# Scanning every second token: decay moved into the rotation tables, and complex products summed on VectorE

## The chip, the cores and the metric

The kernel runs on one core of a Trainium2 chip. The metric is the device time of one execution in microseconds (us). The core's engines work side by side, each through its own list of instructions in order: TensorE (PE in the profile, with its weight loads as PEld), VectorE (DVE), ScalarE (ACT), GpSimd (POOL) and SyncE (SP, which here only issues transfers). Matrix products land in PSUM, and ACT or DVE copies them out into SBUF before the bank can be used again.

## The reference

The input `x` has 2048 tokens of 1024 channels. Two branches read it and a gate mixes them:

```python
g = sigmoid((x * gate_w).sum(-1, keepdims=True))          # one gate per token
# branch a: a spectral filter
a = irfft2(rfft2(x) * (w_r + 1j * w_i))                   # over tokens and channels
# branch b: a diagonal state space model with 1024 complex states
Lam_bar = exp(dt * Lam)                                   # dt = exp(log_dt), one per state
Bu = x @ B_bar.T                                          # B_bar = ((Lam_bar - 1) / Lam) * B
h[t] = Lam_bar * h[t - 1] + Bu[t]                         # 2048 steps, complex
b = 2 * real(h @ C.T) + x * Dskip
out = g * a + (1 - g) * b
```

## The kernel before

**Order of work.** Nothing is scheduled by the compiler. Every stage is a generator that issues a few instructions and yields, and the string `ORDER` (L57) names by one letter each which generator goes on next. The recurrence is cut into closures collected in `work`; the letter `v` takes the next of them, by the list `PIECES` (L44). `SLOTS` (L52) says which of four PSUM slots each product takes. So each engine's list is written out by hand, and an instruction that waits holds all that stands behind it on its engine.

**Branch b.** The 2048 tokens are eight chunks c0 to c7 of 256. For each chunk `unit_mm` (L391) makes B times x on PE, four groups per chunk, and `unit_out` (L402) copies each group on ACT into the tile `h`, which holds real and imaginary part, 8 blocks of 128 states and 256 tokens. `recur` (L334) then solves the recurrence in place on DVE. A complex decay is a rotation times a real radius: the kernel turns Bu back by the angle of each token (`cross(1)`, `along(0)`, `join_re`, `join_im`: two products with tables of sines and cosines and two sums), so that only the real radius is left, runs a first-order scan over the tokens with it (`scan`, L361, once for the real and once for the imaginary part, 8 blocks of 256 tokens in a row, with a zero radius in front of each block), and turns the result forward again with tables that also hold the factor of B_bar (`cross(3)`, `along(2)`, `out_re`, `out_im`). Between chunks three small operations carry the last state over (`carry_part`, `carry_sum`, `carry_in`). c0 and c1 are worked in two halves of four blocks each (their scans are over 1024 elements), c2 to c7 whole (2048 elements).

The tables come from `make_tab` (L272) in four steps of two blocks each: angles and their reduction on DVE or ACT, sine and cosine on ACT, casts of these into `tab` 1 and 0 on POOL or ACT, scaled copies `t1` and `t2` on ACT, and four operations on DVE that write `tab` 2 and 3. `radii` (L266) fills the scan's radii `rz` on POOL.

A finished chunk feeds `early_mm` (L732, letter n) or `own_mm` (L866, letter o): PE multiplies it with C, 128 tokens at a time, and ACT scales the result by 1 - g. The first ten token tiles go to memory and are added to the other branch there; the last ones are finished in SBUF.

**Branch a.** The transform over channels is `fold`, `fd`; over tokens it is made in two factors with a turn through memory (`s1`, `s1_store`, then `load_mid`, `s2`). `s2_out` (L599) copies the spectrum into `X2`. `times_w` (L612) multiplies it with W on DVE: for each of 8 groups and 2 halves one operation makes all four real products (W's real and imaginary part times the spectrum's). They are not summed there: `is1` (L621), the first factor of the inverse transform, sums them on PE by taking all four as inputs, with four versions of its cosines and sines in `MT`: 32 matmuls for each group, eight running at once in parts of the array. `is1_out`, `is1_store`, `load_last`, `is2` and `is2_out` (L665, into `ZT`) finish the tokens' inverse transform, and `spectral_mm` to `spectral` (L800 to L847) that over channels.

## Time and profile before

| | |
|---|---|
| median of 3 runs | 305.39 us (304.64 to 305.44) |
| span of the profiled execution | 303.6 us |
| PE busy | 296.4 us, 98% |
| DVE busy | 289.3 us, 95% |
| ACT busy | 188.5 us, 62% |
| POOL busy | 73.3 us, 24% |
| granted PE clock | 0.999 |

The profiled execution's own time is its span from the first to the last instruction; the runs are timed from outside and hold what lies around it too, 1.8 us between the two figures. A row of the profile that groups instructions reads: line, engine, operation, output <- inputs, shapes (partitions x elements, type), count | busy us, mean ns of one | idle us of the engine in front of them, and what ended it. A row of the time line reads: start, duration, engine, line, operation, and in brackets the idle time before it. Several equal instructions in a row are merged, with their count.

### The profile page before, as it was taken

What the parts mean: (1) busy time and instruction counts of PE and PEld (TensorE: products, weight loads), DVE (VectorE), ACT (ScalarE), POOL (GpSimd) and SP (SyncE); (2) the same over time, 40 slices, a digit from 0 to 9 for tenths busy, and PEclk for the clock granted to TensorE, in tenths of its full rate; (3) what the DMA queues carried; (4) which work ended last, traced back from release to release, by engine and by line L of the source; (5) the groups of instructions that cost most, each with busy time, mean ns of one, the idle gap of its engine ahead of it and who ended that gap; (6) DMA issues with size and microseconds to landing.
All of it is one profiled execution on the core that took longest, in us unless ns stands there. A gap on an engine that the chain in (4) does not pass through costs nothing. (4 is left out here: it accounts for less than half of the span.)

```text
span 303.6 us, 6402 instructions
## 1 busy us (share of the span) xinstructions
PE 296.4 (98%) x2568; PEld 197.4 (65%) x2592; DVE 289.3 (95%) x340; ACT 188.5 (62%) x255; POOL 73.3 (24%) x99
## 2 busy tenths in 40 slices
PE   8999999999999999999999999999999999999995
PEld 5664677878864685458553866669657986645543
DVE  2999999999999999999999999999899999999995
ACT  4999999896532383667665865529668774343400
POOL 2100420745893001110210220202011253252330
PEclk9999999999999999999999999999999999999999
DMA  6999999989999599895948798687758876978976
GB/s 208 341 201 194 253 193 310 162 142 154 268 214 241 160 259 219 181 250 189 212 96 258 163 223 225 139 294 147 242 174 185 165 88 135 160 132 143 165 153 181
DMA packets 74157, 59.35 MB, mean 196 GB/s; under 512 B 44904, under 2 KB 61680, under 8 KB 74128
## 3 DMA queue, kind: packets, MB, share of 16 engines
q1 hardware_dynamic: 66560, 49.82, 65.8%
q0 software_dynamic: 6912, 8.69, 23.0%
q10 hardware_dynamic: 656, 0.44, 0.5%
q8 instruction: 20, 0.33, 0.4%
q14 instruction: 9, 0.07, 0.1%
HBM read 27.46 MB, written 23.08 MB: 166 GB/s over the span
## 5 line engine op out<-in xcount | busy, mean ns | idle before, releaser
L398 PE MATMUL psu<-xQ,BT 128*128 128x256 bf16 x1024 | 116.5, 273 | 0.2 <-DVE X L449 0.2
L398 PEld LDWEIGHTS <-BT 128*128 128x128 bf16 x1024 | 99.0, 98 | 17.3 <-issue 4.6
L713 PE MATMUL ps_y<-CT,h 128*128 128x512 bf16 x397 | 92.5, 379 | 0.9
L363 DVE TENSOR_TENSOR_SCAN h<-rz,h 128x2048 bf16<-128x2048 f32 (+1 forms) x20 | 70.8, 3561 | 0.0
L713 PEld LDWEIGHTS <-h 128*128 128x128 bf16 x416 | 39.6, 98 | 46.3 <-issue 2.9
L785 POOL DMA_DIRECT2D y_scratch<-su x20 | 17.3, 902 | 135.7 <-ACT su L779 105.4
L408 ACT CAST h<-psu 128x1024 bf16<-128x1024 f32 x32 | 32.3, 1011 | 18.7 <-PE psu L398 13.1
L350 DVE TENSOR_TENSOR h<-h,tab 128x4096 bf16<-128x4096 bf16 (+1 forms) x20 | 37.1, 1859 | 0.1
L744 ACT ACTIVATE ye<-ps_y,omg 128x512 f32<-128x512 f32 x26 | 17.9, 689 | 26.3 <-PE ps_y L713 11.8
L347 DVE TENSOR_TENSOR xQ<-h,tab 128x4096 bf16<-128x4096 bf16 x12 | 27.4, 2284 | 1.0 <-ACT h L408 1.0
L603 ACT CAST X<-ps_s 128x1024 bf16<-128x1024 f32 x16 | 16.2, 1010 | 14.6 <-PE ps_s L594 11.2
L727 PE MATMUL ps_q<-CT,h 128*128 128x512 bf16 (+2 forms) x110 | 21.3, 348 | 0.2
L817 ACT ACTIVATE BT<-ps_id,gB 128x1024 bf16<-128x1024 f32 x14 | 15.3, 1114 | 9.9 <-PE ps_id L810 5.7
L671 ACT CAST ZT<-ps_is 128x1024 bf16<-128x1024 f32 x16 | 15.8, 1017 | 6.2 <-PE ps_is L661 6.2
L637 ACT CAST C<-ps_is 128x1024 bf16<-128x1024 f32 x16 | 15.7, 1011 | 5.1 <-DMA xQ<-in_A_x_dram 3.4
L851 POOL DMA_DIRECT2D BT<-y_scratch x10 | 13.1, 1452 | 19.7 <-DVE BT L846 13.3
L727 PEld LDWEIGHTS <-h 128*128 128x128 bf16 x112 | 10.3, 98 | 10.4 <-DVE h L378 0.5
L779 ACT ACTIVATE su<-xs,omg 128x512 f32<-128x512 bf16 x20 | 14.2, 723 | 4.1 <-DMA y_scratch<-su 2.2
L929 ACT COPY xQ<-pt 128x1024 bf16<-128x1024 bf16 x12 | 12.2, 1082 | 1.3 <-PE pt L919 1.3
L449 ACT CAST X<-ps_fd 128x1024 bf16<-128x1024 f32 x12 | 12.3, 1062 | 1.0 <-PE ps_fd L439 0.9
L617 DVE TENSOR_TENSOR UV<-X,Wb 128x2048 bf16<-128x2048 bf16 x8 | 9.6, 1220 | 0.6 <-ACT ye L744 0.6
L617 DVE TENSOR_TENSOR UV<-X,raw 128x2048 bf16<-128x2048 bf16 x8 | 9.8, 1223 | 0.2 <-ACT X L604 0.2
(200 smaller groups left out, 397.3 us busy)
## 6 DMA issues: line engine op xcount, KB each, us to landing
y_scratch<-ye SPq DMA_DIRECT2D x20, 256.0 KB, 4.6
y_scratch<-su POOLq DMA_DIRECT2D x20, 256.0 KB, 4.7
Bb<-turn_scratch SPq DMA_DIRECT2D x16, 256.0 KB, 5.2
turn_scratch<-C SPq DMA_DIRECT2D x16, 256.0 KB, 4.1
raw<-turn_scratch SPq DMA_DIRECT2D x8, 512.0 KB, 4.3
xs<-in_A_x_dram SPq DMA_DIRECT2D x13, 256.0 KB, 3.9
out_dram<-BT SPq DMA_DIRECT2D x11, 256.0 KB, 4.3
CT<-in_A_x_dram SPq DMA_DIRECT2D x5, 512.0 KB, 6.1
```

What stands on the lines that cost most here:

```text
L347: nc.vector.tensor_mul(out=tmps["s"], in0=u[:, ::-1], in1=bc(i))
L350: nc.vector.tensor_mul(out=u, in0=u, in1=bc(i))
L363: nc.vector.tensor_tensor_scan(out=seg, data0=rz[:, js.start + j:js.start + j + m].rearrange("p j t -> p (j t)"), data1=seg, initial=0.0, ...
L398: nc.tensor.matmul(psu[:, j, :], lhsT=BT[4 * q + j][:, ri, d8, :], rhs=xQ[:, c, d8, :], start=(d8 == 0), stop=(d8 == 7))
L408: nc.scalar.copy(out=hs[c][:, ri, 4 * q:4 * q + 4].rearrange("p b (q j) -> p b q j", j=32), in_=psus.pop((c, q, ri)).rearrange("p b (j q) ...
L603: nc.scalar.copy(out=X2, in_=ps2s[g][b])
L617: nc.vector.tensor_mul(out=UV, in0=X2s.pop((g, b)).unsqueeze(1).to_broadcast([P, 2, 2, K]), in1=fft["Wb"][g // 2 % 2][:, :, at:at + 1, :]. ...
L671: nc.scalar.copy(out=ZT[:, 4 * kp:4 * kp + 4, :, 4 * G:4 * G + 4].rearrange("p (c r) n g -> p c r n g", c=2), in_=pszs.pop((G, kp)).rearra ...
L713: nc.tensor.matmul(psy, lhsT=hs[c][:, ri, jb, P * tq:P * (tq + 1)], rhs=CT[ri][:, jb, 512 * dh:512 * (dh + 1)], start=(i == 0), stop=(i == ...
L727: nc.tensor.matmul(psq, lhsT=hs[c][:, ri, jb, P * tq:P * (tq + 1)], rhs=CT[ri][:, jb, at:at + n], start=(i == 0), stop=(i == 15))
L744: nc.scalar.activation(out=ye, in_=psys[tb][:, K * hf:K * (hf + 1)], func=ACT.Copy, scale=omg[:, tb:tb + 1])
L785: nc.gpsimd.dma_start(out=y_dram[tb, hf], in_=xgs[tb, hf], accum_op=ALU.add)
```

## The change

**Recurrence.** The tokens of a chunk are kept as 128 even ones and 128 odd ones (first index of the new `h`). The rotation tables for odd tokens are multiplied by the inverse radius on the way in and by the radius on the way out, so that a pair's two tokens need no decay between them. `fold_in` adds the even tokens to the odd ones, `scan` runs over the 128 odd tokens only, with the squared radius, and `next_` (on ACT, eight scaled copies per chunk, two to a piece) multiplies each odd result by the squared radius and writes it one place on, from where `fill_in` adds it to the next even token. The carry is put into the first place of the same buffer (`carry_in`) and added to the odd token (`carry_add`). For whole chunks real and imaginary part are now one scan of 2048 elements; for halves there are two of 512.

**Tables.** `make_tab` lets POOL cast sine and cosine of the even tokens together and multiply those of the odd ones by the inverse radius for `tab` 0 and 1, and by the radius in place for the tables 2 and 3.

**Products with W.** One operation per group makes the four products for both halves (4096 elements); a subtraction and an addition on DVE sum them, and `is1` takes the two sums: 16 matmuls a group, and `MT` keeps three versions. `X2` and `UV` are one buffer of double size instead of two.

**Layout.** Token tiles hold the even or the odd tokens of a chunk, so rows of `x` and `out`, the gate and `ZT` are laid out by that. `PIECES`, `SLOTS` and `ORDER` are written anew.

```diff
-        MT=b16(np.concatenate([-np.cos(angM), -np.sin(angM), np.cos(angM), np.sin(angM)], axis=2)),
+        MT=b16(np.concatenate([-np.sin(angM), np.cos(angM), np.sin(angM)], axis=2)),
...
     def radii():
         for jb in range(8):
-            nc.gpsimd.tensor_copy(out=rz[:, jb, :], in_=r_sb[:, jb:jb + 1].to_broadcast([P, TC]))
-            nc.gpsimd.memset(rz[:, jb, 0:1], 0.0)
+            nc.gpsimd.tensor_copy(out=rz[:, :, jb, :], in_=r2_sb[:, jb:jb + 1].unsqueeze(1).to_broadcast([P, 2, TS]))
+            nc.gpsimd.memset(rz[:, :, jb, 0:1], 0.0)
...
         yield from sincos(tmp, ang, sh, sn_f, cs_f, "rot")
         yield
-        cast(2 * jp)(out=tab[:, 1, js, :], in_=sn_f)
-        yield
+        nc.gpsimd.tensor_copy(out=tab[:, 0:2, 0, js, :], in_=sc[:, :, :, 0:TS])
+        yield
+        for j in range(2):
+            jb = 2 * jp + j
+            odd = sc[:, :, j, TS:TC]
+            nc.gpsimd.tensor_scalar_mul(out=tab[:, 0:2, 1, jb, :], in0=odd, scalar1=rinv[:, jb:jb + 1])
+            nc.gpsimd.tensor_scalar_mul(out=odd, in0=odd, scalar1=r_sb[:, jb:jb + 1])
+            yield
...
-        cast(2 * jp + 1)(out=tab[:, 0, js, :], in_=cs_f)
...
-        sh = [P, 2, n, TC]
-        u = hs[c][:, :, js, :]
+        sh = [P, 2, 2, n, TS]
+        u = hs[c][:, :, :, js, :]
...
-        def carry_in():
-            on_in.tensor_add(out=u[:, :, :, 0], in0=u[:, :, :, 0], in1=carry[:, :, js])
+        def carry_in():
+            first = tmps["s"][:, 0, :, :, 0]
+            if c:
+                nc.vector.tensor_add(out=first, in0=ck[:, :, 0, js], in1=ck[:, :, 1, js])
+            else:
+                nc.vector.memset(first, 0.0)
+
+        def carry_add():
+            nc.vector.tensor_add(out=u[:, 1, :, :, 0], in0=u[:, 1, :, :, 0], in1=tmps["s"][:, 0, :, :, 0])
+
+        def fold_in():
+            nc.vector.tensor_add(out=u[:, 1], in0=u[:, 1], in1=u[:, 0])
...
-        def scan(ri, j, m):
-            seg = u[:, ri, j:j + m].rearrange("p j t -> p (j t)")
-            nc.vector.tensor_tensor_scan(out=seg, data0=rz[:, js.start + j:js.start + j + m].rearrange("p j t -> p (j t)"),
-                                         data1=seg, initial=0.0, op0=ALU.mult, op1=ALU.add)
+        def scan():
+            flat = lambda t, i: t[:, i, js].rearrange("p j t -> p (j t)") if n < 8 else t.rearrange("p r j t -> p (r j t)")
+            for i in range(2 if n < 8 else 1):
+                seg = flat(hs[c][:, 1], i)
+                nc.vector.tensor_tensor_scan(out=seg, data0=flat(rz, i), data1=seg, initial=0.0, op0=ALU.mult, op1=ALU.add)
+
+        def next_(j):
+            for i in range(j, j + 2):
+                nc.scalar.activation(out=tmps["s"][:, 0, :, i, 1:TS], in_=u[:, 1, :, i, 0:TS - 1], func=ACT.Copy,
+                                     scale=r2_sb[:, js.start + i:js.start + i + 1])
+
+        def fill_in():
+            nc.vector.tensor_add(out=u[:, 0], in0=u[:, 0], in1=tmps["s"][:, 0])
...
         work.extend((lambda: cross(1), lambda: along(0), join_re, join_im))
+        work.append(carry_in)
         if c:
-            work.append(carry_in)
-        work.extend((lambda: scan(0, 0, n), lambda: scan(1, 0, n)))
+            work.append(carry_add)
+        work.extend((fold_in, scan))
         if c + 1 < NCH:
-            work.extend((carry_part, carry_sum))
+            work.append(carry_part)
+        work.extend(partial(next_, j) for j in range(0, n, 2))
+        work.append(fill_in)
         work.extend((lambda: cross(3), lambda: along(2), out_re, out_im))
...
     def times_w():
         for g in range(8):
-            for b in range(2):
-                UV = UVs[g, b] = fft["gt"].tile([P, 2, 2, K], BF16, name="UV", tag="guv", bufs=2)
-                at = 2 * (g % 2) + b
-                nc.vector.tensor_mul(out=UV, in0=X2s.pop((g, b)).unsqueeze(1).to_broadcast([P, 2, 2, K]),
-                                     in1=fft["Wb"][g // 2 % 2][:, :, at:at + 1, :].to_broadcast([P, 2, 2, K]))
-                yield
+            UV = UVs[g] = fft["gt"].tile([P, 2, 2, 2, K], BF16, name="UV", tag="guv", bufs=1)
+            W = fft["Wb"][g // 2 % 2][:, :, 2 * (g % 2):2 * (g % 2) + 2]
+            nc.vector.tensor_mul(out=UV, in0=X2s.pop(g).unsqueeze(1).to_broadcast([P, 2, 2, 2, K]),
+                                 in1=W.unsqueeze(2).to_broadcast([P, 2, 2, 2, K]))
+            yield
+            nc.vector.tensor_sub(out=UV[:, 0, 0], in0=UV[:, 0, 0], in1=UV[:, 1, 1])
+            yield
+            nc.vector.tensor_add(out=UV[:, 0, 1], in0=UV[:, 0, 1], in1=UV[:, 1, 0])
+            yield
...
     def is1():
         for g in range(8):
             psc = pscs[g] = [psum([P, 2, K], "ps_is1") for _ in range(2)]
-            UV = [UVs.pop((g, b)) for b in range(2)]
-            for i, (u, r, n) in enumerate(((0, 0, 64), (0, 1, 32), (1, 0, 32), (1, 1, 0))):
+            UV = UVs.pop(g)
+            for r in range(2):
                 for c in range(4):
                     rows = slice(32 * c, 32 * (c + 1))
                     for b in range(2):
-                        nc.tensor.matmul(psc[c // 2][64 * b:64 * (b + 1), c % 2, :], lhsT=fft["MT"][rows, 2 * g + b, n:n + 64],
-                                         rhs=UV[b][rows, u, r, :], start=(i == 0), stop=(i == 3), tile_position=(32 * c, 64 * b))
+                        nc.tensor.matmul(psc[c // 2][64 * b:64 * (b + 1), c % 2, :], lhsT=fft["MT"][rows, 2 * g + b, 32 - 32 * r:96 - 32 * r],
+                                         rhs=UV[rows, 0, r, b, :], start=(r == 0), stop=(r == 1), tile_position=(32 * c, 64 * b))
             yield
...
+        nc.scalar.activation(out=r2_sb, in_=are, func=ACT.Exp, scale=2.0)
+        nc.scalar.activation(out=rinv, in_=are, func=ACT.Exp, scale=-1.0)
```

The cosines' factor in `rot` (the carry) takes the squared radius too, and the exponent of the radius is kept from below -60 ln 2 so that its inverse stays finite.

The new order between a scan and its `fill_in`, on DVE: in c2 the product with W of group 3 and `along(0)` of c3, with small sums; in c3 `cross(1)` and `along(0)` of c4 and the product of group 5; in c4 the same of c5 and the product of group 7; in c5 `cross(1)`, `along(0)` and both joins of c6; in c6 `cross(3)` and `along(2)` of c5; in c7 eight operations of the spectral sums. On ACT the `next_` pieces of c6 stand behind four copies of `is2`.

151 lines of the change are left out of this document (75 added, 76 removed), and 13 rows, old and new, of the table PIECES.

## The prediction

> **What bounds the kernel now.** I read the totals of the page first, then the busy time in five stretches whose bounds are events of the kernel: the tables finish at about 80 us, the products with W run from 104.7 to 188.8, the row-wise inverse transform from 188.8, the spectral sums from 241. The columns are PE, PEld, DVE, ACT, POOL, then granted clock, DMA share, GB/s.
>
> ```profile
> PE 296.4 (98%) x2568; PEld 197.4 (65%) x2592; DVE 289.3 (95%) x340; ACT 188.5 (62%) x255; POOL 73.3 (24%) x99
> ...
> 0.00:80.00 80.00, 77.20 (x691) 56.85 (x695) 72.27 (x136) 69.92 (x98) 26.14 (x56) 1.00 1.10 218
> 80.00:104.70 24.70, 24.54 (x193) 15.10 (x193) 24.04 (x33) 7.15 (x12) 12.29 (x8) 1.00 0.93 213
> 104.70:188.80 84.10, 83.73 (x837) 52.34 (x829) 83.30 (x66) 54.79 (x79) 8.69 (x10) 1.00 0.85 208
> 188.80:241.00 52.20, 51.94 (x466) 37.34 (x470) 51.15 (x33) 33.44 (x42) 6.86 (x8) 1.00 0.75 191
> 241.00:303.60 62.60, 58.98 (x403) 35.73 (x407) 58.58 (x77) 23.19 (x26) 19.28 (x18) 1.00 0.82 146
> ```
>
> Two engines are full at once. PE is idle for 303.6 - 296.4 = 7.2 us, 2.8 of it in the first stretch and 3.6 in the last; DVE for 14.3 us. The clock is 1.00 throughout, so PE's time is work. ACT has 115 us free, but only 10 of the first 80. The chain of waits shows the same balance: it runs through DVE's last chunk of the recurrence, then through PE to the end.
>
> ```profile
> 285.42 1.15 DVE h L378
> ...
> 286.61 5.79 PE ps_q L727 x26
> ...
> 292.44 7.99 PE ps_q L727 x52
> ...
> 300.46 0.35 DVE raw L899
> ```
>
> So a microsecond taken from PE alone, or from DVE alone, is not necessarily a microsecond off the end. What both lose counts.
>
> **The price list for DVE.** Rows of single instructions include about 0.09 us in which the next one already runs. The true step is the second instruction of a pair: the merged pair less the single.
>
> ```profile
> L363 DVE TENSOR_TENSOR_SCAN h<-rz,h 128x2048 bf16<-128x2048 f32 x12 | 52.7, 4416 | 0.0
> L363 DVE TENSOR_TENSOR_SCAN h<-rz,h 128x1024 bf16<-128x1024 f32 x8 | 18.1, 2278 | 0.0
> L350 DVE TENSOR_TENSOR h<-h,tab 128x4096 bf16<-128x4096 bf16 x12 | 27.4, 2287 | 0.0
> L617 DVE TENSOR_TENSOR UV<-X,raw 128x2048 bf16<-128x2048 bf16 x8 | 9.8, 1223 | 0.2 <-ACT X L604 0.2
> L617 DVE TENSOR_TENSOR UV<-X,Wb 128x2048 bf16<-128x2048 bf16 x8 | 9.6, 1220 | 0.6 <-ACT ye L744 0.6
> L846 DVE TENSOR_TENSOR BT<-BT 128x1024 bf16<-128x1024 bf16 x7 | 4.7, 684 | 0.0
> ```
>
> ```profile
> 73.61 4.46 DVE L363 TENSOR_TENSOR_SCAN h<-rz,h 128x1024 bf16<-128x1024 f32 x2
> ...
> 148.37 2.34 DVE L617 TENSOR_TENSOR UV<-X,Wb 128x2048 bf16<-128x2048 bf16 x2
> ...
> 175.20 8.74 DVE L363 TENSOR_TENSOR_SCAN h<-rz,h 128x2048 bf16<-128x2048 f32 x2
> ...
> 191.51 4.49 DVE L350 TENSOR_TENSOR h<-h,tab 128x4096 bf16<-128x4096 bf16 x2
> ...
> 278.92 1.29 DVE L846 TENSOR_TENSOR BT<-BT 128x1024 bf16<-128x1024 bf16 x2
> ```
>
> Scan of 2048: 8.74 - 4.42 = 4.32. Scan of 1024: 4.46 - 2.28 = 2.18; by the line through both, a scan of 512 is 1.11. Two-tensor bf16 operation: 4096 elements 4.49 - 2.29 = 2.20; 2048 1.12; 1024 1.29 - 0.69 = 0.60. An element of a scan costs four times one of a sum, which is what the change trades on.
>
> **Recurrence, DVE.** Six chunks (c2 to c7) run whole. Each loses two scans of 2048 and gets one, and adds fold_in and fill_in over 2048 elements: -4.32 + 2 x 1.12 = -2.08, six times -12.5. The first two run in halves, four in all: two scans of 1024 become two of 512 and two sums of 1024 are added: -2 x 2.18 + 2 x 1.11 + 2 x 0.60 = -0.94, four times -3.8. The four table products and four joins keep their element counts; their innermost runs stay contiguous, so I keep their price. The carry keeps three small operations (new: into the first column, add, part). Recurrence: -16.3 us.
>
> **Products with W, DVE.** Sixteen products of 2048 go, 16 x 1.12 = 17.9. Eight products of 4096 with a subtraction and an addition of 1024 each come, 8 x (2.20 + 2 x 0.60) = 27.2. That is +9.3 us, all in the stretch 104.7 to 188.8, where only about three chunks (-2 each) repay it. DVE over the whole kernel: -16.3 + 9.3 = -7.0 us, but in that stretch it is about +3.
>
> **PE.** is1 issues half its matmuls, since the complex sum is already made.
>
> ```profile
> L629 PE MATMUL ps_is<-UV,raw 32*64 32x512 bf16 x256 | 8.6, 380 | 0.0
> ...
> 132.92 1.07 PE L629 MATMUL ps_is<-UV,raw 32*64 32x512 bf16 x32
> ```
>
> Eight tiles run side by side, so 32 matmuls take 1.07 us; half are 0.5, and eight groups save 8.6 / 2 = 4.3. Halved groups may keep a fixed edge (1.07 contains one matmul's 0.38 of latency): 8 x 0.5 = 4.0 is the other bound. I take -4.2. No other matmul changes in count or size.
>
> **ACT.** The 64 instructions of next_ scale 254 elements each; nearest row: a scaled copy of 256. Its pair gives 0.94 - 0.54 = 0.40, single 0.54. Three casts go to POOL.
>
> ```profile
> L292 ACT ACTIVATE t<-sn_f,ci 128x256 f32<-128x256 f32 x8 | 3.8, 543 | 0.0
> ...
> L294 ACT CAST tab<-cs_f 128x512 bf16<-128x512 f32 x2 | 1.2, 610 | 0.0
> ...
> L287 ACT CAST tab<-sn_f 128x512 bf16<-128x512 f32 x1 | 0.6, 617 | 0.0
> ```
>
> ```profile
> 45.36 0.94 ACT L292 ACTIVATE t<-sn_f,ci 128x256 f32<-128x256 f32 x2
> ```
>
> 64 x 0.40 = 25.6, less 1.8: +24 us (+33 by the single). ACT goes to about 212 us, 70%; in the stretch of the W products from 54.8 to about 66 of 84. It fits; the cost is not its sum but the new hand-off: scan (DVE), next_ (ACT), fill_in (DVE). One chunk's eight take 3.3 us. In the written order DVE has work between scan and fill_in: in c2 to c5 at least two products of 4096 (4.4 us) and sums besides; in c7 four of the spectral sums and some more, about 4 us. Cover is thus 1 us or more in most chunks, nearly nothing in c6 and c7, where next_ stands behind copies of PSUM. If those two slip by 0.4 us each, that is 0.8. If the cover were gone everywhere, 8 x 3.3 = 26 us. What waits behind a next_ that itself waits for the scan is the copying of h, X, C and ZT out of PSUM, and so PE's next free bank.
>
> **POOL and the tables.** Each of the four table steps gets one cast of 1024 elements and four products of 256; five casts of 512 go.
>
> ```profile
> L268 POOL COPY rz<-r_sb 128x256 f32<-128x256 f32 x8 | 4.5, 559 | 0.3 <-ACT r_sb L1091 0.3
> ...
> L287 POOL CAST tab<-sn_f 128x512 bf16<-128x512 f32 x3 | 2.4, 805 | 24.0 <-ACT sn_f L1111 24.0
> ...
> L294 POOL CAST tab<-cs_f 128x512 bf16<-128x512 f32 x2 | 1.2, 614 | 0.9 <-ACT cs_f L1113 0.9
> ```
>
> A product of 256 by the copy of 256 (scaled ones are not in the trace): 0.56, sixteen 9.0; four casts of 1024 at twice 0.6: 4.8; less 3.6: +10 us of POOL. It has the room, but the chain is longer: ACT's t1 and t2, DVE's last four table operations and cross1 now all stand behind POOL, about 3.4 us per table. And POOL does not run freely beside DVE:
>
> ```profile
> 86.38 1.21 DVE L350 TENSOR_TENSOR h<-h,tab 128x2048 bf16<-128x2048 bf16 x1
> 87.52 2.27 DVE L363 TENSOR_TENSOR_SCAN h<-rz,h 128x1024 bf16<-128x1024 f32 x1
> ...
> 90.90 2.27 DVE L347 TENSOR_TENSOR xQ<-h,tab 128x4096 bf16<-128x4096 bf16 x1
> 93.40 0.19 DVE L557 CAST Zp<-zps 128x32 bf16<-128x32 f32 x1 [0.23 <-PE zps L553]
> ```
>
> ```profile
> 86.39 6.90 POOL L540 TENSOR_TENSOR AB<-Wh 128x32 f32<-128x32 f32 x1
> ```
>
> A POOL sum of 32 elements started with DVE's L350 and ended 6.9 us later, when DVE paused at 93.2. The other way, DVE pays: its sum of 1024 beside two POOL operations took 1.11 instead of 0.68.
>
> ```profile
> 30.10 0.68 DVE L943 TENSOR_TENSOR preT<-xQ 128x1024 bf16<-128x1024 bf16 x1
> 30.70 1.11 DVE L945 TENSOR_TENSOR sums<-xQ 128x1024 bf16<-128x1024 bf16 x1
> ```
>
> ```profile
> 30.65 0.61 POOL L287 CAST tab<-sn_f 128x512 bf16<-128x512 f32 x1 [11.45 <-ACT sn_f L1111]
> ```
>
> The Trainium skill, "SBUF — State Buffer", section "Who interferes with whom", says why: a DVE instruction with two SBUF inputs and a POOL instruction that reads SBUF exclude each other for a whole instruction. These rows agree. By that rule taken in full, POOL's 10 us more would be 10 us of DVE, and the change would cost DVE 3 us instead of saving 7.
>
> From rows: for two POOL operations (0.61 + 0.86) DVE lost 0.43, a third; of 10 us that makes about 3; bounds 0 and 10. The loss falls before 80 us. There the order leaves PE cover: the first matmul of the output (n) stands behind all of c0 and also behind DVE's first six operations of c1a (two products, two joins, fold, scans: about 6.5 us). So I put no PE time on it, and DVE's balance at -7.0 + 3 = -4.0, about PE's -4.2.
>
> **Layout moves.** Splitting even and odd tokens in h, ZT and the rows of x and out changes strides, not counts: h is read by PE in runs of 128 as before, the copies keep 1024 elements, each DMA row stays 2 KB. The three transposes of x stand far ahead of their use. I price all of these at nothing, bound -0.5 to +1.5 us. X2 and UV become one buffer each instead of two halves, so the product of group g+1 waits until is1 of g is done; the order puts a scan or other DVE work between, and is1 takes 0.5 us.
>
> **The sum.** The execution profiled spans 303.6 us; the median of the runs is 305.39, 1.8 more, taken as fixed. PE -4.2, hand-offs +0.8: 303.6 - 3.4 = 300.2 span, 302.0 as a time.
>
> **Rivals.**
> (1) Both engines gain more: with DVE ahead, PE's inner idle shrinks too. DVE's last write starts at 300.46 and the span ends at 303.6, so about 3.2 of PE's 7.2 idle us are the tail; if two thirds of the other 4.0 vanish and hand-offs cost nothing, 305.4 - 4.2 - 2.6 = 298.6. For it: DVE is the last to release in the chain. Against: three new hand-offs.
> (2) DVE sets the pace in the W stretch, and POOL's claim on it is paid in full in the table stage: two thirds to all of the 10 us leave DVE with -0.3 to +3, and if PE then only follows DVE, 305.1 to 308.4; nearest the low end, 305.5, since part of the table stage's DVE work reads PSUM. For it: L540. Against: the third that the row at 30.70 gives, and the 6.5 us of PE's cover.
> (3) The other side: ACT's next_ blocks. ACT works in order; next_ cannot start before the scan ends, and copies out of PSUM stand behind it, so PE loses its banks. There are ten scan units (four halves, six chunks). From 4.2 / 10 = 0.42 us of PE lost per unit it eats the whole gain, from 0.51 it is slower. With one single next_ pair of lateness per unit, 0.94 us: 305.4 - 4.2 + 9.4 = 310.6; with 0.7, 308.2. For it: PE at 98% has no time to lose. Against: ACT has 115 us free.
> (4) The change does not do what it says: the 4096 product with W repeats each input by a broadcast and could run at half rate, 8 x 2.20 = 17.6 us more on DVE in its tightest stretch: about 315. The old product has the same kind of broadcast at 1220 ns for 2048, so hardly.
>
> **How the numbers follow.** Forecast 302.0 (with 300.5 to 304 around it): 0.56. Rival 1, 298.6: 0.12. Rival 2, 305.5: 0.16. Rival 3, 308: 0.14. Rival 4: 0.02. About 0.3% (0.9 us) is what a measurement of this kernel can tell from no change. Faster takes the forecast and rival 1 and some of rival 2: 0.71. Same: most of rival 2, 0.13. Slower: rivals 3, 4 and the upper end of 2, 0.16. The range runs from rival 1's 298.6 to 306.5, above rival 2 and short of most of rival 3.
>
> **What would show it.** PE's busy time near 292 and is1 near 4.3 us; six scans of 2048 and eight of 512 elements, together about 36 us instead of 70.8; products with W at 2.3 us each; PE idle no more than about 8 us. ACT's waits for DVE h in front of next_, and PE's waits for ACT behind them, show rival 3; long POOL products and DVE waiting for POOL before 80 us show rival 2. I am wrong if PE's idle time grows by more than 3 us.

## The result: 3.5% slower, and the profile after

| | before | after |
|---|---|---|
| median of the runs shown | 305.01 us (304.54 to 305.44) | 315.95 us (314.75 to 317.05) |
| ratio | | 1.0349, 95% interval 1.0310 to 1.0387 |
| span of the profiled execution | 303.6 us | 313.9 us |

The forecast was 302.0 us in a range of 298.6 to 306.5: wrong in sign. In e9 and e10 below one run of ten (345.77 us at a granted clock of 0.853, 306.52 us at 0.994) is left out of median and ratio. First the totals of the page after, with PE's busy tenths and granted clock in 40 slices:

```profile
span 313.9 us, 6252 instructions
...
PE 298.3 (95%) x2464; PEld 197.3 (63%) x2464; DVE 287.7 (92%) x364; ACT 212.5 (68%) x318; POOL 83.0 (26%) x114
...
PE   8999799978999999997999999999999999999994
...
PEclk9999979999999999999999999999999999999999
```

PE's idle time was 303.6 - 296.4 = 7.2 us and is now 313.9 - 298.3 = 15.6. DVE's went from 14.3 to 26.2. The work itself hardly changed: PE +1.9, DVE -1.6. Of the 10.3 us, 8.4 are waiting on PE's side. (PE's busy time did not fall by what is1 lost. Some matmuls ran at a lower clock, below, and the trace of before lacks 24 of its 2592 matmul records: e9's trace, with the same work on PE and all records, has PE busy for 298.1 us and idle for 6.0.) The same five stretches as in the prediction, of the kernel after (PE, PEld, DVE, ACT, POOL, clock, DMA share, GB/s):

```profile
0.00:80.00 80.00, 71.30 (x616) 51.23 (x616) 64.49 (x129) 63.73 (x94) 40.39 (x66) 0.98 1.02 207
80.00:104.70 24.70, 24.70 (x201) 16.80 (x200) 23.94 (x39) 13.65 (x22) 7.59 (x12) 1.00 0.84 185
104.70:188.80 84.10, 81.84 (x720) 50.87 (x719) 80.21 (x77) 58.38 (x94) 8.70 (x10) 1.00 0.87 210
188.80:241.00 52.20, 52.20 (x433) 34.44 (x431) 51.55 (x37) 41.60 (x65) 6.02 (x7) 1.00 0.74 194
241.00:313.90 72.90, 68.27 (x503) 43.98 (x500) 67.46 (x86) 35.17 (x46) 20.28 (x19) 1.00 0.79 142
```

In the first 80 us PE did 71.30 us of work instead of 77.20, and DVE 64.49 instead of 72.27. From 80 to 241 us PE is never idle but for one hole between 104.7 and 188.8: what is lost early has no room to be made up later.

The groups that the change touches:

```profile
L370 DVE TENSOR_TENSOR_SCAN h<-rz,h 128x2048 bf16<-128x2048 f32 x6 | 26.5, 4420 | 0.1
L370 DVE TENSOR_TENSOR_SCAN h<-rz,h 128x512 bf16<-128x512 f32 x8 | 9.3, 1209 | 0.1
L634 DVE TENSOR_TENSOR UV<-X,raw 128x4096 bf16<-128x4096 bf16 x4 | 9.1, 2280 | 0.2 <-PE ps_is L650 0.2
L650 PE MATMUL ps_is<-UV,raw 32*64 32x512 bf16 x128 | 5.1, 386 | 0.0
L374 ACT ACTIVATE xQ<-h,r_sb 128x254 bf16<-128x254 bf16 x48 | 20.5, 505 | 6.6 <-DVE h L370 6.6
L291 POOL TENSOR_SCALAR tab<-sc,rinv 128x256 bf16<-128x256 f32 x8 | 10.5, 1307 | 0.0
L292 POOL TENSOR_SCALAR sc<-sc,r_sb 128x256 f32<-128x256 f32 x8 | 9.6, 1197 | 0.8
L299 ACT ACTIVATE t<-sc,ci 128x256 f32<-128x256 f32 x16 | 7.3, 503 | 7.7 <-POOL sc L292 7.7
L303 DVE SCALAR_TENSOR_TENSOR tab<-sc,cr,t 128x256 bf16<-128x256 f32 x8 | 4.0, 505 | 4.0 <-ACT t L299 4.0
```

The change does what it says: the scans take 35.8 us instead of 70.8, is1 5.1 instead of 8.6. What is out of line are the products on POOL, 1.2 to 1.3 us each, and the column behind the second bar: ACT waited 7.7 us for them, and DVE 4.0 us for ACT. How that reaches PE is seen in the time line of one table step, first POOL, then ACT, then PE:

```profile
31.64 0.61 POOL L286 CAST tab<-sc 128x512 bf16<-128x512 f32 x1 [7.44 <-ACT sc L1139]
32.23 1.36 POOL L291 TENSOR_SCALAR tab<-sc,rinv 128x256 bf16<-128x256 f32 x1
33.69 0.97 POOL L292 TENSOR_SCALAR sc<-sc,r_sb 128x256 f32<-128x256 f32 x1
34.64 1.82 POOL L291 TENSOR_SCALAR tab<-sc,rinv 128x256 bf16<-128x256 f32 x1
36.56 0.92 POOL L292 TENSOR_SCALAR sc<-sc,r_sb 128x256 f32<-128x256 f32 x1
37.43 0.40 POOL L267 COPY rz<-r_sb 128x256 f32<-128x256 f32 x1
```

```profile
34.70 0.51 ACT L299 ACTIVATE t<-sc,ci 128x256 f32<-128x256 f32 x1 [0.31 <-POOL sc L292]
37.52 1.31 ACT L299 ACTIVATE t<-sc,ci 128x256 f32<-128x256 f32 x3 [2.31 <-POOL sc L292]
38.73 0.99 ACT L491 CAST CT<-ps_s 128x1024 bf16<-128x1024 f32 x1
```

```profile
33.58 3.67 PE L412 MATMUL psu<-xQ,BT 128*128 128x256 bf16 x32
37.08 0.38 PE L991 MATMUL ps_r<-preT,JP_sb 128*128 128x512 bf16 x1
39.77 5.32 PE L412 MATMUL psu<-xQ,BT 128*128 128x256 bf16 x32 [2.31 <-ACT CT L491]
```

POOL's chain of one cast and four products lasts from 31.64 to 37.48, 5.8 us. ACT's second scaled copy stands 2.31 us for its last product; behind it in ACT's list stands a copy out of PSUM (L491) that has nothing to do with tables; PE needs that bank and stands 2.31 us too. The next 32 matmuls then took 5.32 us, where the 32 before the wait took 3.67: another 1.65. Two of the other three table steps do the same to PE: at 66.42 us it has stood 1.92 us for a copy L491, and at 78.07 us 1.34 us for a copy L463, each behind scaled copies that waited for POOL (1.67 and 2.14 us).

The second hole, between 136 and 149 us, runs through a store. ACT's copy C waits for the place of an earlier store to memory, and the shifted copies of c2 stand behind it:

```profile
139.15 0.90 ACT L374 ACTIVATE xQ<-h,r_sb 128x254 bf16<-128x254 bf16 x2
143.48 1.01 ACT L658 CAST C<-ps_is 128x1024 bf16<-128x1024 f32 x1 [3.42 <-DMA turn_scratch<-C]
144.38 0.91 ACT L374 ACTIVATE xQ<-h,r_sb 128x254 bf16<-128x254 bf16 x2
```

```profile
144.54 3.65 PE L412 MATMUL psu<-xQ,BT 128*128 128x256 bf16 x32 [1.05 <-ACT C L658]
149.05 7.15 PE L412 MATMUL psu<-xQ,BT 128*128 128x256 bf16 x64 [0.85 <-ACT X L621]
```

DVE's `fill_in` of c2 starts at 148.13 after 3.06 us of idling for them. PE stands 1.05 us for the copy C and 0.85 us for the copy X that is behind the shifted ones.

### The profile page after: what moved, and what is told of

It reads as the page before. It is cut to its first block, busy times and chain, and to the rows that moved or that the text cites. A ratio compares the mean times of both kernels' runs of the same rounds, so it can differ in the third digit from the quotient of the medians.

```text
span 313.9 us, 6252 instructions
## 1 busy us (share of the span) xinstructions
PE 298.3 (95%) x2464; PEld 197.3 (63%) x2464; DVE 287.7 (92%) x364; ACT 212.5 (68%) x318; POOL 83.0 (26%) x114
## 4 chain that ended last, share of the span: by engine, by line
PE 43%; ACT 12%; issue 12%; DVE 12%; POOL 10%; DMA 8%; SPq 1%; POOLq 0%; ACTq 0%; DVEq 0%
PE psu L412 18%; PE ps_y L734 15%; PE ps_q L748 6%; POOL tab L291 3%; ACT xQ L950 3%; POOL sc L292 2%; DVE h L345 2%; DVE xQ L342 2%; DMA y_scratch<-su 2%; DMA turn_scratch<-C 2%; DMA BT<-y_scratch 2%; DMA out_dram<-BT 2%; ACT X L463 2%; DVE h L370 1%; PE ps_s L611 1%
## 5 line engine op out<-in xcount | busy, mean ns | idle before, releaser
L412 PE MATMUL psu<-xQ,BT 128*128 128x256 bf16 x1024 | 117.8, 275 | 6.5 <-ACT CT L491 2.3
L412 PEld LDWEIGHTS <-BT 128*128 128x128 bf16 x1024 | 100.2, 99 | 24.9 <-issue 11.9
L734 PE MATMUL ps_y<-CT,h 128*128 128x512 bf16 x416 | 93.6, 379 | 0.0
L806 POOL DMA_DIRECT2D y_scratch<-su x20 | 19.7, 996 | 129.2 <-ACT su L800 101.3
L370 DVE TENSOR_TENSOR_SCAN h<-rz,h 128x512 bf16<-128x512 f32 (+1 forms) x14 | 35.9, 2585 | 0.2
L374 ACT ACTIVATE xQ<-h,r_sb 128x254 bf16<-128x254 bf16 x48 | 20.5, 505 | 6.6 <-DVE h L370 6.6
L692 ACT CAST ZT<-ps_is 128x1024 bf16<-128x1024 f32 x16 | 16.7, 1127 | 3.0 <-PE ps_is L683 3.0
L838 ACT ACTIVATE BT<-ps_id,gB 128x1024 bf16<-128x1024 f32 x14 | 15.1, 1113 | 5.2 <-PE ps_id L831 3.8
L748 PEld LDWEIGHTS <-h 128*128 128x128 bf16 x112 | 10.3, 98 | 11.0 <-issue 0.7
L299 ACT ACTIVATE t<-sc,ci 128x256 f32<-128x256 f32 x16 | 7.3, 503 | 7.7 <-POOL sc L292 7.7
L342 DVE TENSOR_TENSOR su<-h,tab 128x2048 bf16<-128x2048 bf16 x8 | 9.8, 1228 | 2.9 <-POOL tab L291 2.8
```

The costliest lines, as they stand in the source:

```text
L342: nc.vector.tensor_mul(out=tmps["s"], in0=u[:, :, ::-1], in1=bc(i))
L370: nc.vector.tensor_tensor_scan(out=seg, data0=flat(rz, i), data1=seg, initial=0.0, op0=ALU.mult, op1=ALU.add)
L374: nc.scalar.activation(out=tmps["s"][:, 0, :, i, 1:TS], in_=u[:, 1, :, i, 0:TS - 1], func=ACT.Copy, scale=r2_sb[:, js.start + i:js.start + ...
L412: nc.tensor.matmul(psu[:, j, :], lhsT=BT[4 * q + j][:, ri, d8, :], rhs=xQ[:, c, d8, :], start=(d8 == 0), stop=(d8 == 7))
L692: nc.scalar.copy(out=fft["ZT"][:, kp, :, :, 2 * G:2 * G + 2], in_=pszs.pop((G, kp)).rearrange("p v (x n) -> p x n v", n=64))
L734: nc.tensor.matmul(psy, lhsT=hs[c][:, tq, ri, jb, :], rhs=CT[ri][:, jb, 512 * dh:512 * (dh + 1)], start=(i == 0), stop=(i == 15 and tb not ...
```

## The experiments

### Which engine sets the pace?

The prediction counted on both PE and DVE. So work was taken from each alone in the kernel before, then from both, and from DVE in the kernel after.

```diff
 e8 (before, is1)
-            for i, (u, r, n) in enumerate(((0, 0, 64), (0, 1, 32), (1, 0, 32), (1, 1, 0))):
+            for i, (u, r, n) in enumerate(((0, 0, 64), (0, 1, 32))):
 e9 (before) and e16 (after), mul_skip; e10 = e8 and e9 together
-                nc.vector.tensor_mul(out=xs[tb], in0=xs[tb], in1=fft["Db"])
```

> The kernel before with half of is1's matmuls left out (the products with W's imaginary part are not added), 16 instead of 32 for each group, and nothing else changed: PE's gain of the change by itself, without anything on DVE. Theory PE (PE sets the pace, the step of the prediction that counted -4.2 us): 300.5 to 301.5 us. Theory DVE (DVE sets the pace, as the kernel with only W changed says: 9.8 us more on DVE, 8.6 us more in all): 304.3 to 305.5, no change.

> The kernel before with the 13 VectorE products of x by Dskip left out (that part of the output is missing), nothing else: VectorE loses 7.8 us, spread from 160 to 230 us, TensorE loses nothing. Theory A (VectorE sets the pace of the kernel before): about 298. Theory B (TensorE sets it): 305. Theory C (both are full and each stretch is set by whichever is late there): between, about 302, since the half of is1's products left out of TensorE gave 2.7 of its 4.

> The kernel before with both cuts at once: half of is1's matrix products and all 13 products by Dskip left out. Theory C: more than the two alone together, because where one engine is freed the other one was the limit: 305 less 2.7 less what the Dskip products gave alone, less some 1 to 3 us more, about 297 to 299. Theories A and B: the sum of the two alone, no more.

> The kernel after without the 13 VectorE products by Dskip (that part of the output is missing): VectorE loses 7.8 us between 160 and 230 us. If VectorE sets the pace of the kernel after behind the tables: 308 to 311. If TensorE does, as in the kernel before: within 1.5 us of 316.

| | median | ratio to before |
|---|---|---|
| e8: PE loses half of is1 | 302.96 us | 0.9909 (0.9879 to 0.9940) |
| e9: DVE loses 13 products | 305.90 us | 1.0036 (1.0001 to 1.0072) |
| e10: both | 302.11 us | 0.9889 (0.9866 to 0.9912) |
| e16: after, DVE loses 13 products | 315.24 us | 1.0332 (1.0292 to 1.0371) |

The result is e9's theory B, that PE sets the pace, for both kernels; e8 alone came out between its two theories. Is1's group of matmuls went from 8.6 to 5.6 us in e8, and 0.0091 x 305.7 = 2.8 us came off the end: nearly one for one. DVE's row in e9 says 282.3 us busy instead of 289.3, and nothing came off; both cuts together gave 0.0111 x 305 = 3.4 us, no more than PE's alone within the intervals. In e16 DVE's 7.6 us less bought nothing either. These products lie between 160 and 230 us, so this shows that DVE's sum of work is not a bound there; it does not show that DVE may be late anywhere (below).

### The products on POOL

```diff
 e1 (after): the odd rows are only cast
-        for j in range(2):
-            nc.gpsimd.tensor_scalar_mul(out=tab[:, 0:2, 1, jb, :], in0=odd, scalar1=rinv[:, jb:jb + 1])
-            nc.gpsimd.tensor_scalar_mul(out=odd, in0=odd, scalar1=r_sb[:, jb:jb + 1])
+        nc.gpsimd.tensor_copy(out=tab[:, 0:2, 1, js, :], in_=sc[:, :, :, TS:TC])
 e5 (after): the products on DVE, all four of a table where POOL's last stood
-            nc.gpsimd.tensor_scalar_mul(out=tab[:, 0:2, 1, jb, :], in0=odd, scalar1=rinv[:, jb:jb + 1])
-            nc.gpsimd.tensor_scalar_mul(out=odd, in0=odd, scalar1=r_sb[:, jb:jb + 1])
+            nc.vector.tensor_scalar_mul(out=tab[:, 0:2, 1, jb, :], in0=odd, scalar1=rinv[:, jb:jb + 1])
+            nc.vector.tensor_scalar_mul(out=odd, in0=odd, scalar1=r_sb[:, jb:jb + 1])
```

> The changed kernel with its 16 scaled products on POOL left out: the odd half of the first two tables is only cast (four casts of 512 elements), so the decay inside a pair is left out of all four tables. Everything else, the order too, is that of the changed kernel (315.95 us). Theory POOL (the loss is made before 85 us, by products that take 0.92 to 1.98 us each and hold ACT's t1, the copies out of PSUM behind it, and so PE): PE's idle time between 28 and 82 us (about 8 us) and the 1.7 us of a slowed clock go, so 306 to 308 us. Theory ACT (the loss is next_ and its hand-offs): the stall before 85 us is a side show that later slack takes up, 314 to 316. Theory W (the extra sums of the products with W on DVE set the pace of the middle): same, 314 to 316.

> The changed kernel with the 16 scaled products of the tables made by DVE in place of POOL, all four of a table step at the place of the last POOL product; nothing is left out. DVE pays 16 times about 0.27 us (the spacing of its scaled copies of 256 elements), 4.3 us, before 75 us. Theory POOL: 308 to 311, since the wait goes and DVE's 4.3 us come, part of them in time that DVE stood waiting. Theories ACT and W: 315 to 319, since DVE has more to do and nothing else changes.

e1: 310.8 us, ratio 1.0154 (1.0078 to 1.0231). e5: 315.54 us, ratio 1.0312 (1.0237 to 1.0386). The stretch from 28 to 82 us in the kernels before, after, e1 and e5, one fence each:

```profile
28.00:82.00 54.00, 53.81 (x492) 42.73 (x491) 52.89 (x80) 46.52 (x68) 24.06 (x39) 1.00 1.12 211
```

```profile
28.00:82.00 54.00, 47.66 (x415) 37.03 (x413) 45.00 (x74) 42.28 (x65) 30.72 (x40) 0.97 1.01 190
```

```profile
28.00:82.00 54.00, 52.31 (x479) 41.84 (x477) 51.77 (x82) 48.33 (x73) 18.30 (x33) 1.00 1.05 213
```

```profile
28.00:82.00 54.00, 48.96 (x439) 38.24 (x438) 51.75 (x92) 45.37 (x69) 12.54 (x28) 1.00 1.05 201
```

Without the products PE works 4.65 us more in this stretch, the clock is back at 1.00, and the end comes (1.0349 - 1.0154) x 305 = 5.9 us earlier by the ratios (5.2 by the medians). That is about half of the loss (a third to four fifths within the intervals), and it is shown; the expectation of 306 to 308 us had counted on more. None of the three waits of PE behind scaled copies is left in e1's trace: from 28 to 82 us PE stands only for two loads, 1.12 us for c_T and 0.49 us for B. DVE hardly gains: with 3.6 us of casts in place of 20.1 us of products on POOL it is busy for 287.3 us instead of 287.7.

Moving the products to DVE (e5) did not give the 308 to 311 us expected of it. In its trace ACT waits for them 2.9 us instead of 7.7, and PE's waits for the copies L492 behind them are 0.63 us each, where the copies L491 of after had cost 2.31 and 1.92. But a product takes 0.45 us on DVE, not the 0.27 expected, and DVE is busy for 4.6 us more. PE does 48.96 us of work in the stretch, still 4.85 less than before, and its longest wait is now another, 1.84 us for the load of c_T. So e5 took away most of the chain's waits and paid for it elsewhere; it does not tell the chain's length from the engine that holds it.

### The shifted copies on ACT

```diff
 e2 (after), e12 (e1) and e18 (e17): the copies left out
-        work.extend(partial(next_, j) for j in range(0, n, 2))
+        work.extend((lambda: None) for j in range(0, n, 2))
 e17 (e1): the letter L, the load of K, moved in ORDER
-YccvncvLsyM
+YLccvncvsyM
```

> The changed kernel without next_: the 64 scaled copies on ACT are left out, so fill_in adds what the buffer holds and the even tokens lack their predecessor's state. Theory POOL: the 27 us of ACT time are mostly hidden; only the 3 us stall at 145 us and small change go, 312 to 316. Theory ACT: the hand-off is the loss, 304 to 307. Theory W: 314 to 316.

> The kernel after without the 16 scaled POOL products (odd rows of the tables only cast) and without ScalarE's 64 shifted copies (the even rows take in a stale buffer): both suspected hand-offs are gone, the output is not the reference's. If what was left of the loss with the products out (310.8) is the shifted copies': 305 to 307. If the engines' fullness and the order set it: within 1 us of 310.8.

> The kernel after without POOL's 16 scaled products, with the load of K issued ahead of the last three transposing transfers of C before it. If that load's place only mattered in the run without shifted copies: 310.8 as with the products out alone. If the load's place cost something there too: 308 to 310.

> The same, and without ScalarE's 64 shifted copies. If the shifted copies and their hand-offs hold the rest of the loss: 305 to 307, 3 us or more under the kernel with them. If they cost nothing, as with the products in: within 1.5 us of the kernel with them; the rest of the loss then belongs to the order of work, and is not settled further.

e2: 316.13 us, ratio 1.0352 (1.0268 to 1.0435): 64 copies, 24 us of ACT and every hand-off from the scan to ACT gone, and no time with them. PE's work from 110 to 150 us rose from 37.74 to 39.16, so the second hole closes for the most part, but the end does not move: 1.1 us of this is lost again near the end, where PE's wait for ACT's copy BT (L838) grew from 0.6 to 1.7 us.

e12, with the products gone too, took 313.22 us (ratio 1.0249, 1.0188 to 1.0310), no better than e1. The trace of its slowest run (315.1 us) shows a stall of its own: first SyncE's queue, then PE.

```profile
85.45 5.05 SPq L720 DMA_TRANSPOSE CT<-in_B_C_im_dram  x1
90.55 1.31 SPq L720 DMA_TRANSPOSE CT<-in_B_C_re_dram  x1
92.03 0.45 SPq L511 DMA_DIRECT2D K_sb<-c_K  x1
```

```profile
94.78 0.36 PE L567 MATMUL zps<-Bcol,K_sb 32*128 32x32 bf16 x8 [2.67 <-DMA K_sb<-c_K]
96.41 0.37 PE L608 MATMUL ps_s<-Bb,KRS_sb 64*32 64x512 bf16 x1 [1.27 <-DMA Bb<-turn_scratch]
97.34 1.05 PE L608 MATMUL ps_s<-Bb,KRS_sb 64*32 64x512 bf16 x15 [0.56 <-DMA Bb<-turn_scratch]
```

A transposing transfer of C took 5.05 us to issue, its neighbours 1.3; the small load of K stood behind it, and PE stood 4.5 us in all. With that load put ahead, e17 took 312.04 us (1.0209, 1.0145 to 1.0273) and e18 310.72 us (1.0189, 1.0118 to 1.0260): the same within the intervals. So no share of the rest of the loss is shown for the shifted copies, though up to about 3 us could hide in this noise.

### The products with W

```diff
 e4 (before, its own order): one pair tile of one buffer, the sums, 16 matmuls a group
+            UV = UVs[g] = fft["gt"].tile([P, 2, 2, 2, K], BF16, name="UV", tag="guv", bufs=1)
...
+                if b == 1:
+                    nc.vector.tensor_sub(out=UV[:, 0, 0], in0=UV[:, 0, 0], in1=UV[:, 1, 1])
+                    nc.vector.tensor_add(out=UV[:, 0, 1], in0=UV[:, 0, 1], in1=UV[:, 1, 0])
 e14 (before): the pair tile without the sums, 32 matmuls a group
+            UV = UVs[g] = fft["gt"].tile([P, 2, 2, 2, K], BF16, name="UV", tag="guv", bufs=1)
 e15 (before): two buffers; for each product its own two sums, 16 matmuls
+                if g >= 4:
+                    nc.vector.tensor_sub(out=UV[:, 0, 0], in0=UV[:, 0, 0], in1=UV[:, 1, 1])
+                    nc.vector.tensor_add(out=UV[:, 0, 1], in0=UV[:, 0, 1], in1=UV[:, 1, 0])
 e13: as e15 in all groups, with nc.gpsimd for nc.vector
```

> The kernel before with only the products with W changed: the four products as before in two operations of 2048 elements, behind the second of them the subtraction and the addition on DVE, and 16 matmuls instead of 32 for each group. The order is that of before. DVE gets 16 x 0.60 = 9.6 us more between 104 and 189 us, PE 3.5 to 4.2 us less. If DVE sets the pace in that stretch (theory W): 311 to 315 us. If PE sets it: 301 to 302. If both do in turn, as theory POOL needs for the middle of the changed kernel: 306 to 311.

> The kernel before with the two products of a group of W in one tile of a single buffer, as the sums would need it, but without the sums: 32 matrix products for a group as before. VectorE and TensorE work as before. If the single buffer caused the loss of 8.6 us of the products with W alone: 309 to 314. If VectorE's added work caused it: 305 to 306.

> The kernel before with VectorE's complex sums only in the last four of the eight groups, each of the two products of a group with its own buffer and its own two sums (512 elements, by my estimate from 0.69 us for 1024 about 0.37 us each, +6 us of VectorE), and 16 instead of 32 matrix products in those groups (half of the 2.7 us that the removed products gave). If VectorE has the slack that leaving out the Dskip products showed: 303.5 to 305. If VectorE's work counts in full: 308 to 311.

> The kernel before with the complex sums in all eight groups made by POOL (32 operations of 512 elements, estimated at 1 to 2 us each from its scaled products of 0.92 us for 256 and its casts of 1.04 for 1024), two buffers, 16 matrix products a group. VectorE's work is as before. If only VectorE's work mattered: 302 to 304. If the delay in the chain to the products or POOL's claim on SBUF matters: 306 to 315.

| | median | ratio to before |
|---|---|---|
| e4 | 313.65 us | 1.0250 (1.0172 to 1.0329) |
| e14 | 305.32 us | 0.9997 (0.9983 to 1.0012) |
| e15 | 310.51 us | 1.0166 (1.0122 to 1.0210) |
| e13 | 344.35 us | 1.1262 (1.1245 to 1.1280) |

The single buffer costs nothing (e14). DVE's sums cost, in the order of before: half of them add 5.9 us to DVE (289.3 to 295.2) and 0.0166 x 305.6 = 5.1 us to the end, although PE has less to do. The rows of before and of e15 for the stretch from 150 to 210 us, and PE's wait in e15:

```profile
150.00:210.00 60.00, 59.68 (x571) 39.25 (x562) 59.20 (x40) 35.80 (x53) 7.76 (x9) 1.00 0.76 196
```

```profile
150.00:210.00 60.00, 55.23 (x452) 34.41 (x442) 59.76 (x53) 31.41 (x47) 6.01 (x7) 0.97 0.76 183
```

```profile
L635 PE MATMUL ps_is<-UV,raw 32*64 32x512 bf16 x192 | 8.2, 402 | 4.4 <-DVE UV L620 4.4
```

DVE was full there before, 59.20 of 60, and is full now; what it does more, PE waits for (4.4 us in front of is1). In the same stretch and later, taking DVE work away bought nothing (e9). DVE's full stretch has slack in one direction only. The sums also stand between a product and the is1 that needs it; whether DVE's fullness or this place in the chain makes PE wait, e4 and e15 do not separate. And the wait belongs to the order of before: in after's trace PE never waits for UV, so e4's loss is no part of after's.

On POOL the sums are far worse (e13, expected at 315 us at most):

```profile
L621 POOL TENSOR_TENSOR UV<-UV 128x512 bf16<-128x512 bf16 x16 | 43.5, 2716 | 0.0
L620 POOL TENSOR_TENSOR UV<-UV 128x512 bf16<-128x512 bf16 x16 | 39.4, 2465 | 37.5 <-DVE UV L617 23.7 <-DMA raw<-c_MT 12.4 <-DVE carry L371 1.4
```

In the mean that is 2.5 and 2.7 us for 512 elements, where DVE took 0.42 in e15; single ones took 1.15 to 5.27. PE waited 25.5 us for them (18.3 and 7.2). DVE, with the same work as before, was busy for 312.8 us instead of 289.3, beside 80 us more of POOL (153.7 instead of 73.3).

### The recurrence alone

```diff
 e3 (after): the products with W and is1 undone, the order of after
-            nc.vector.tensor_mul(out=UV, in0=X2s.pop(g).unsqueeze(1).to_broadcast([P, 2, 2, 2, K]),
-                                 in1=W.unsqueeze(2).to_broadcast([P, 2, 2, 2, K]))
+            for b in range(2):
+                nc.vector.tensor_mul(out=UV[:, :, :, b], in0=X2[:, :, b].unsqueeze(1).to_broadcast([P, 2, 2, K]),
+                                     in1=W[:, :, b:b + 1].to_broadcast([P, 2, 2, K]))
...
-            for r in range(2):
+            for i, (u, r, n) in enumerate(((0, 0, 64), (0, 1, 32), (1, 0, 32), (1, 1, 0))):
 e6 (e3): POOL's products left out as in e1
 e7 (e3): complete tables; DVE scales the odd rows, POOL makes 8 products
+            nc.vector.tensor_scalar_mul(out=odd, in0=odd, scalar1=r_sb[:, jb:jb + 1])
...
-        nc.scalar.activation(out=rinv, in_=are, func=ACT.Exp, scale=-1.0)
+        nc.scalar.activation(out=rinv, in_=are, func=ACT.Exp, scale=-2.0)
 e11 (e7): ORDER, PIECES and SLOTS of before; all shifted copies of a chunk in
 one piece; in half chunks DVE operations in their place
+                for i in range(n):
+                    nc.vector.scalar_tensor_tensor(out=u[:, 0, :, i, 1:TS], in0=u[:, 1, :, i, 0:TS - 1],
+                                                   scalar=r2_sb[:, js.start + i:js.start + i + 1], in1=u[:, 0, :, i, 1:TS],
+                                                   op0=ALU.mult, op1=ALU.add)
```

> The changed kernel with the products with W undone: two products of 2048 elements for each group, no subtraction or addition, 32 matmuls of is1 and four versions of its table; recurrence, tables, layout and order are those of the changed kernel (315.95 us). DVE gets about 10 us less, PE 3.5 to 4.2 more. Theory DVE: 306 to 308 us. Theory PE: 318 to 320. If the order's other hand-offs set the pace: 313 to 316.

> As the kernel with only the recurrence changed, and the 16 scaled products of the tables on POOL left out too (the odd half is only cast, so the decay inside a pair is missing from the tables): the recurrence's worth without its tables' price. Theory DVE: 10 us below the changed kernel without these products (310.8), 300 to 303, and below before. Theory PE: 313 to 315.

> As the kernel with only the recurrence changed, with the tables complete but built otherwise: DVE multiplies the odd half by the radius in place (8 products, about 0.3 us each, +2.4 us), and POOL makes the first two tables from that with the inverse radius squared (8 products instead of 16), so that ACT's t1 and t2 no longer wait for POOL. Nothing is left out. Theory DVE: between the two others, 303 to 306: POOL's share of the wait is halved and DVE pays 2.4 us. If POOL's products still hold DVE at cross1 as long as before: 306 to 309.

> The recurrence over odd tokens with complete tables (VectorE multiplies the odd half by r, POOL makes 8 scaled products), in the order of work of the kernel before: its list of issues, its list of recurrence pieces and its PSUM slots; the products with W as before. In the four half chunks the shifted addition is 16 VectorE operations with a scalar in place of ScalarE's copies, as the second buffer does not fit there. Nothing is left out. Theory order (the loss of 8.7 us seen with the same tables and the order of after comes from the order being fitted to other costs): 301 to 306. Theory operations (the work of the change itself, hand-offs and small dependent VectorE operations, costs it): 310 to 315. VectorE busy about 285 in both.

| | median | ratio to before |
|---|---|---|
| e3 | 318.60 us | 1.0423 (1.0369 to 1.0476) |
| e6 | 314.85 us | 1.0286 (1.0235 to 1.0336) |
| e7 | 314.35 us | 1.0284 (1.0230 to 1.0338) |
| e11 | 342.26 us | 1.1198 (1.1151 to 1.1246) |

With DVE at 279.5 us in e3, ten less than before, the kernel is 2.7 us slower than after by the medians, with intervals that overlap a little. That fits an order in which PE's matmuls of is1 count, as in e8, and DVE's relief does not. Splitting the table products between DVE and POOL (e7) is worth as much as leaving them out (e6). e6 came out where PE's pace had put it, e7 above both of its ranges (303 to 309 us). e11 failed as a test of a better home for the recurrence, but it shows what after's order is for. Its waits:

```profile
ACT xQ L374 <- DVE h L370: 19.4, 4, 7.3
DVE xQ L342 <- ACT h L445: 11.0, 3, 6.3
DVE h L378 <- ACT xQ L374: 9.8, 2, 7.0
```

The shifted copies put where the second scan stood make ACT wait 19.4 us in four places; copies out of PSUM stand behind them, and DVE stands 11.0 us for those. PE's idle time was 341.5 - 310.5 = 31 us. e11 also differs in the half chunks and in the tables' place in the list, so it does not price the shifted copies alone.

## Why the prediction was wrong, step by step

**"A product of 256 by the copy of 256: 0.56."** This is the step that failed first. The scaled products took 0.92 us at the least and 1.25 in the mean; their starts in the time line, 0.87 to 1.92 us apart, say the same, while the copies of 256 in the same trace took 0.39 to 0.83, 0.57 in the mean. The chain of a table, put at 3.4 us, took 5.3 to 7.0. The copy was the wrong neighbour, and no other was looked for. (The cast in this chain was counted with 1024 elements; it has 512 and took 0.78 us in the mean instead of 1.2, so the products lost more than the chain shows.) POOL's total rose by 9.7 us, as forecast, but by luck: products and casts are 19.6 us more, and the rest of POOL's work happened to take 9.9 us less, 4.5 of it in one sum of 32 elements (L557, 2.4 us where L540 had 6.9).

**"So I put no PE time on it."** This is the step that cost most. The cover that was named, the output matmuls behind DVE's first operations of c1, was the wrong place to look. The late tables reached PE by ACT's list: the scaled copies t1 and t2 wait for POOL, and unrelated copies out of PSUM stand behind them. e1 gives the price, 5 to 6 us where nothing had been put. The prediction had named just this path for the shifted copies (rival 3) and not for t1 and t2, which stand in the same list.

**"PE -4.2, hand-offs +0.8."** The products explain 5.2 us of the 14 between forecast and result; e1, without them, is still 8.8 us above the forecast. The sum had 0.8 us for all new waits of PE, and the new order of the whole had no term at all. In e1's trace PE's waits with a named cause add up to 7.8 us, in before to 2.7. New are 2.0 us in the second hole for the copies C and X, 1.6 for the loads of c_T and B, 0.5 for Bb, and 1.5 near the end for ACT's copy BT, which itself waits 1.96 us for an earlier store to out.

**"What both lose counts."** PE's part held in the main: -4.2 was forecast, is1 gave 3.5 us in after's trace, and e8 shows that such a cut comes off the end nearly one for one. DVE's part did not: 7.0 us off DVE were worth nothing by themselves (e9), so DVE's balance was no ground for a gain; and DVE's +9.3 in the W stretch was a danger that a balance over the whole kernel hid, though it came true only in the order of before (e4: +7.6 us by its ratio, e15: +5.1). In after's order the recurrence's relief does lie beside the sums: undoing them (e3) costs 2.7 us by the medians.

**DVE -7.0.** It came as -1.6. The large terms were right: scans -35.0 against -34.5, the products with W 9.1 + 9.1 + 5.5 + 5.5 = 29.2 for 19.4, +9.8 against +9.3. `fold_in` and `fill_in` came to 20.2 us by their rows, where 18.2 had been taken; the other 3.4 us were not traced to single operations. A part of both is the step that was taken from pairs that overlap. Two sums of `fold_in`, each with the operation behind it, all with POOL idle:

```profile
191.15 1.22 DVE L364 TENSOR_TENSOR h<-h 128x2048 bf16<-128x2048 bf16 x1
192.40 4.42 DVE L370 TENSOR_TENSOR_SCAN h<-rz,h 128x2048 bf16<-128x2048 f32 x1
...
216.27 1.22 DVE L364 TENSOR_TENSOR h<-h 128x2048 bf16<-128x2048 bf16 x1
217.41 0.68 DVE L790 TENSOR_TENSOR xs<-xs,Db 128x1024 bf16<-128x1024 bf16 x1
```

The scan at 192.40 reads what `fold_in` wrote and starts 1.25 us behind it; the product at 217.41 does not and starts 1.14 us behind, near the 1.12 of the price list.

**POOL beside DVE.** The third that the prediction took for DVE's loss is near what e13 shows: 23.5 us of DVE for 80 us of POOL. In the table stage, where it was put at 3 us, e1's 0.4 us shows next to nothing. The Trainium skill, "SBUF — State Buffer", section "Who interferes with whom", has the two exclude each other for whole instructions when DVE has two SBUF inputs; the direction agrees, but DVE did not pay POOL's full time here.

**Rival 1** fell with the sign: PE's idle time grew instead of shrinking. **Rival 2** (the table stage and DVE's late stretch) named the right place with the wrong mechanism, POOL's claim on DVE instead of its delay of ACT. **Rival 3** did not decide after (e2), since its order leaves room between scan and `fill_in`, as the prediction reckoned; it shows only in c2, behind a store (the second hole). e11 shows that the waits are long without that room, together with its other changes. **Rival 4** is refuted: 2.28 us for 4096 elements. **Layout**: the pair tile costs nothing (e14); the rest was not tried alone. The sign that was named for being wrong, PE's idle time growing by more than 3 us, is what the trace shows: +8.4.

**What stays open.** With the products out and the load of K in either place the kernel is still 1.5 to 2.1% slower than before, though is1's cut is in it. It is not shown to be the shifted copies (e18) and, with the products still in, not DVE's work from 160 to 230 us (e16). Where it lies is seen in e1's trace, in the waits named above. Without the shifted copies (e18) the wait for C and X falls from 2.0 to 0.5 us, and three others grow: c_T to 2.0, Bb to 1.2, BT to 2.0. Why these loads, stores and copies come late is not shown: that the new order of the whole fits less well than the old one is likely, but no run isolates it. No kernel with all of the computation in it beat the kernel before; e14 came level with it.

## What to carry to other kernels

Where two engines are both near full, find out which one's work comes off the end before trading work between them: here a microsecond off PE was worth 0.9, one off DVE nothing, and one more on DVE in its full stretch, in front of is1, 0.9. Price a step moved to another engine by its place in the lists, not by the room on that engine: what waits for it, and what unrelated work stands behind the waiter. An operation that the trace doesn't hold needs a bound from a neighbour of its own kind; here the copy bounded the scaled product only from below.

## What the runs showed of the hardware that was not expected

- POOL's product of 256 fp32 elements with one factor per partition took 0.92 to 1.98 us, a copy of the same size 0.39 to 0.83; its sum of two bf16 tiles of 512 elements, beside a DVE busy for 91% of the span, took 1.15 us at the least and 2.5 to 2.7 in the mean, DVE's 0.42.
- After a wait of 2.31 us PE ran slower for a while: 32 matmuls in 5.32 us instead of 3.67. After one of 1.92 us it did not. The length of the wait alone does not decide it: in e4, 64 matmuls took 8.83 us after a wait of 2.73 and 7.16 after one of 2.66. The two windows of after with these waits (clock third from the end), and the second wait:

```profile
40.00:50.00 10.00, 10.00 (x76) 7.55 (x74) 7.59 (x14) 7.00 (x12) 6.90 (x9) 0.83 1.09 205
60.00:70.00 10.00, 8.08 (x74) 6.55 (x71) 8.46 (x16) 7.05 (x14) 4.80 (x8) 1.00 1.06 199
```

```profile
66.42 3.65 PE L412 MATMUL psu<-xQ,BT 128*128 128x256 bf16 x32 [1.92 <-ACT A L491]
```

The Trainium skill, "TensorE: Matmul & The Clock Gate", section "Why this matters for your kernels", warns of idle gaps above about 3 us; here a lower clock followed one of 2.31 us already.

- One transposing transfer took 5.05 us to issue on SyncE between others of 1.3 us, and PE stood 2.67 us for a small load behind it (e12).
